# Where a small bonus row is loaded and spread in the first microseconds of an attention and FFN kernel

## The chip, the cores and the metric

The kernel runs on one core of a Trainium2 chip. The metric is device time in microseconds (us), as the median of several executions. A run's time is about 1.7 us longer than the profile's span of the same run. Times are compared with times and spans with spans.

Besides its time, each execution has on record the mean clock that the throttle granted TensorE.

## The reference

An RWKV-like attention with a decay w, a bonus u and a running state, for 4 batches, 8 heads, 768 steps and head width 48. An FFN follows, from width 384 to 2048 and back, over all 3072 tokens.

```python
for t in range(S):
    kt, vt, rt = k[:, :, t], v[:, :, t], r[:, :, t]
    cur = einsum('bhd,bhe->bhde', u[None] * kt, vt)          # the bonus: u counts for step t alone
    y[:, :, t] = einsum('bhd,bhde->bhe', rt, state + cur)
    state = w[None, :, :, None] * state + einsum('bhd,bhe->bhde', kt, vt)
x = y.transpose(0, 2, 1, 3).reshape(B * S, H * D)
h = x @ w_in
out = (h / (1 + exp(-h))) @ w_out
```

## The kernel before

The work is cut into 24 units (6 chunks of 128 steps, 4 batches each). The bonus of a unit is worked out in the natural layout: GpSimd multiplies k by u (`ku`), then r by that (`rku_f`), VectorE sums over the head's width, and the sums scale v. For this, u has to lie on all 128 partitions (`u_bc`). It is loaded as one small row, TensorE turns it to columns (`to_cols`), and four further transposes of the broadcast columns spread it (`to_rows`). The decay's powers, which `p1` multiplies into the transposed r and k, come from the row w, which goes the same way.

```python
    load_row(nc.sync, wrow, w)              # SP's queue
    load(0, (0,), nc.scalar)                # r of unit 0, ScalarE's queue
    load_row(nc.scalar, urow, u)            # u behind it
    load(0, (1,))                           # k of unit 0, SP's queue; all others follow there
    ...
    def spin(n, t=None):                    # dummy matmuls that keep TensorE's clock up
        ...
    spin(6)
    wT = to_cols(wrow, None)
    spin(3)
    ...
    def p1(i, spins=0, mid=()):
        ...
        for t, src in ((tr, rin), (tk, kin)):
            flat = src[n].rearrange("p h d -> p (h d)")
            for p in range(NP):
                nc.tensor.transpose(t[0:PR, p, :], flat[:, 128 * p:128 * p + PR], ident)
            if mid:
                mid.pop(0)()
        ...
    p1(0, mid=[cols_u, rows_u])             # u's columns between r and k, its spreading behind k
    p1(1)
    nat_ku(0)                               # GpSimd
    nat_rk(0)
    win_part(0, 512)                        # GpSimd issues a part of the weights
    nat_ku(1)
    nat_rk(1)
    ...
    p2(0, spins=2)
    bonus_sum(0)                            # VectorE reduces
    bonus_sum(1)
    ...
    p2(1)
    p3y(0)
    ...
    spin(4)
    p3y(1)
    p3e(1)
    spin(1)
    p4(0)
    p1(2)
    ...
```

## Time and profile before

| | before |
|---|---|
| median of 3 runs | 199.02 us (198.54 to 199.46) |
| span of the profile | 197.3 us |
| TensorE busy, idle | 189.2 us, 8.1 us |
| GpSimd's first bonus product starts | 8.19 us |
| its fourth (`rku_f` of unit 1) starts | 12.27 us |
| TensorE idle in 12 to 15 us | 1.81 us |

The change concerns the start, where everything stands behind GpSimd, whose four bonus products wait for `u_bc`. The lines are in the prediction below.

### The profile page before, as it was taken

What the parts mean: (1) busy time and instruction counts of PE and PEld (TensorE: products, weight loads), DVE (VectorE), ACT (ScalarE), POOL (GpSimd) and SP (SyncE); (2) the same over time, 40 slices, a digit from 0 to 9 for tenths busy, and PEclk for the clock granted to TensorE, in tenths of its full rate; (3) what the DMA queues carried; (4) which work ended last, traced back from release to release, by engine and by line L of the source; (5) the groups of instructions that cost most, each with busy time, mean ns of one, the idle gap of its engine ahead of it and who ended that gap; (6) DMA issues with size and microseconds to landing.
All of it is one profiled execution on the core that took longest, in us unless ns stands there. A gap on an engine that the chain in (4) does not pass through costs nothing.

```text
span 197.3 us, 4925 instructions
## 1 busy us (share of the span) xinstructions
PE 189.2 (96%) x1918; PEld 127.4 (65%) x1918; DVE 115.7 (59%) x233; ACT 91.0 (46%) x207; POOL 115.2 (58%) x145
## 2 busy tenths in 40 slices
PE   7969999899899999999999999999999999999993
PEld 2737878787666877675566766557666546644563
DVE  5867658885758764975675686476576344210121
ACT  3464587799311626215961216682016680069300
POOL 4389969989966859697669647735437710000000
PEclk9999999999999999999999999999999999999999
DMA  5999997999788754665567377526371011210022
GB/s 115 220 168 139 145 230 152 174 182 195 152 192 211 163 114 104 146 138 129 119 120 139 103 176 163 104 59 121 94 190 43 20 22 43 79 60 0 3 81 80
DMA packets 89696, 24.12 MB, mean 122 GB/s; under 512 B 82888, under 2 KB 89672, under 8 KB 89672
## 3 DMA queue, kind: packets, MB, share of 16 engines
q1 hardware_dynamic: 84940, 20.46, 48.1%
q0 software_dynamic: 3680, 3.15, 10.7%
q10 hardware_dynamic: 1052, 0.20, 0.5%
q8 instruction: 15, 0.25, 0.5%
q14 instruction: 9, 0.07, 0.1%
HBM read 20.45 MB, written 4.72 MB: 128 GB/s over the span
## 4 chain that ended last, share of the span: by engine, by line
PE 72%; POOL 11%; DMA 9%; issue 3%; SPq 1%; DVE 0%; POOLq 0%
PE ops L373 30%; PE hps L361 24%; DMA kin<-in_k_dram 9%; PE ae L270 8%; PE xs L245 4%; POOL ku L183 3%; POOL rku_f L189 3%; POOL kc L194 2%; PE y L296 2%; POOL win L416 2%; PE y L293 2%; POOL vu L206 1%; PE ops L387 1%; PE sps L312 1%; SPq L69 1%
## 5 line engine op out<-in xcount | busy, mean ns | idle before, releaser
L364 ACT ACTIVATE gT<-hps 128x256 f16<-128x256 f32 (+1 forms) x128 | 59.8, 494 | 50.5 <-PE hps L361 48.9
L361 PE MATMUL hps<-xT,win 128*128 128x256 f16 (+1 forms) x384 | 69.2, 326 | 0.2
L373 PE MATMUL ops<-wout,gT 128*128 128x384 f16 x368 | 63.8, 326 | 0.0
L361 PEld LDWEIGHTS <-win 128*128 128x128 f16 x384 | 35.4, 98 | 22.9 <-issue 0.7
L373 PEld LDWEIGHTS <-gT 128*128 128x128 f16 x368 | 34.7, 98 | 22.4
L279 DVE TENSOR_TENSOR am<-ae,maskM 128x512 f16<-128x512 f32 x24 | 16.6, 691 | 31.9 <-PE ao L272 31.8
L377 DVE COPY osb<-ops 128x384 f32<-128x384 f32 x23 | 12.7, 554 | 28.9 <-PE ops L373 28.7
L183 POOL TENSOR_TENSOR ku<-kin,u_bc 128x384 f32<-128x384 f32 x24 | 24.2, 1006 | 7.0 <-ACT u_bc L152 5.4
L270 PEld LDWEIGHTS ae<-rk 48*128 48x128 f32 x192 | 23.1, 187 | 7.3 <-issue 4.7
L206 POOL TENSOR_TENSOR vu<-vin,rku 128x384 f32<-128x384 f32 x23 | 19.1, 832 | 14.6 <-DVE rku L200 14.5
L272 PE MATMUL ao<-rk 48*128 48x128 f32 x192 | 27.5, 284 | 0.0
L270 PE MATMUL ae<-rk 48*128 48x128 f32 x192 | 27.5, 284 | 0.0
L256 DVE TENSOR_TENSOR rk<-xs,pif 112x512 f32<-112x512 f32 x40 | 25.6, 681 | 1.7 <-PE xs L245 1.7
L262 ACT CAST rT<-rk 112x512 f16<-112x512 f32 x20 | 12.3, 616 | 29.7 <-DVE rk L256 29.7
L189 POOL TENSOR_TENSOR rku_f<-rin,ku 128x384 f32<-128x384 f32 x24 | 24.1, 1004 | 1.9
L194 POOL TENSOR_TENSOR kc<-kin,lamC 128x384 f16<-128x384 f32 x24 | 24.0, 1004 | 0.0
L272 PEld LDWEIGHTS ao<-rk 48*128 48x128 f32 x192 | 23.1, 187 | 0.0
L303 DVE TENSOR_TENSOR y<-y,vu 128x384 f16<-128x384 f32 x24 | 13.4, 557 | 8.3 <-POOL kc L194 2.5
L326 POOL CAST stb<-st 112x384 f16<-112x384 f32 x12 | 6.1, 504 | 20.7 <-DVE st L321 20.7
L279 DVE TENSOR_TENSOR am<-ao,maskM 128x512 f16<-128x512 f32 x24 | 16.3, 680 | 0.0
L200 DVE TENSOR_REDUCE rku<-rku_f 128x8 f32<-128x384 f32 x24 | 13.2, 550 | 3.2 <-POOL rku_f L189 2.7
L296 PE MATMUL y<-v,am 128*128 128x48 f16 x192 | 12.2, 185 | 2.8 <-ACT st L452 1.5
(73 smaller groups left out, 170.5 us busy)
## 6 DMA issues: line engine op xcount, KB each, us to landing
kin<-in_k_dram SPq DMA_DIRECT2D x24, 192.0 KB, 3.4
vin<-in_v_dram SPq DMA_DIRECT2D x24, 192.0 KB, 3.7
rin<-in_r_dram SPq DMA_DIRECT2D x23, 192.0 KB, 3.4
out_dram<-osb SPq DMA_DIRECT2D x23, 192.0 KB, 1.9
win<-in_moe_w_in_dram POOLq DMA_DIRECT2D x4, 384.0 KB, 5.7
wout<-in_moe_w_out_dram POOLq DMA_DIRECT2D x2, 768.0 KB, 11.5
xT<-y SPq DMA_TRANSPOSE x18, 2.3
rin<-in_r_dram ACTq DMA_DIRECT2D x1, 192.0 KB, 2.7
```

The lines of the kernel that those rows point to most:

```text
L183: nc.gpsimd.tensor_tensor(out=L["ku"], in0=kin[i % NIN][:, :, 0:D], in1=u_bc, op=ALU.mult)
L189: nc.gpsimd.tensor_tensor(out=L["rku_f"], in0=rin[i % NIN][:, :, 0:D], in1=L["ku"], op=ALU.mult)
L194: nc.gpsimd.tensor_tensor(out=kc[i % NKC][:, :, 0:D], in0=kin[n][:, :, 0:D], in1=lamC, op=ALU.mult)
L206: nc.gpsimd.tensor_tensor(out=L["vu"], in0=vin[i % NIN], in1=L["rku"].unsqueeze(2).broadcast_to([128, H, D]), op=ALU.mult)
L256: nc.vector.tensor_tensor(out=rk[:, :, :, 64 * g:64 * g + 64], in0=xs[g][0:PR], in1=lam(g), op=ALU.mult)
L270: nc.tensor.matmul(ae[:, p, :], L["kT"][0:D, p, :], L["rT"][0:D, p, :], start=True, stop=True)
L272: nc.tensor.matmul(ao[:, p, :], L["kT"][64:PR, p, :], L["rT"][64:PR, p, :], start=True, stop=True)
L279: nc.vector.tensor_tensor(out=am, in0=a, in1=maskM.unsqueeze(1).broadcast_to([128, NP, C]), op=ALU.mult)
L296: nc.tensor.matmul(y[:, 2 * p + j, :], L["am"][j][:, p, :], v16[:, 2 * p + j, :], start=not sc, stop=(not sc or j == 1))
L361: nc.tensor.matmul(hps, win[:, q, ft * 128:(ft + 1) * 128], xts[sc][:, q, b0:b1, :].rearrange("p b t -> p (b t)"), start=(q == 0), stop=(q ...
L364: nc.scalar.activation(out=gts[sc][:, ft, b0 * C:b1 * C], in_=hps, func=AF.Silu)
L373: nc.tensor.matmul(ops, gts[sc][:, ft, b * C:(b + 1) * C], wout[:, ft, :], start=(ft == 0), stop=(ft == NFT - 1))
```

## The change

The intent is to have u spread before unit 0's own transposes, so that GpSimd starts earlier. u therefore goes first and alone on ScalarE's queue. r of unit 0, now needed later, goes behind w on SP's queue. The diff, cut to its core:

```diff
     load_row(nc.sync, wrow, w)
-    load(0, (0,), nc.scalar)
     load_row(nc.scalar, urow, u)
-    load(0, (1,))
+    load(0, (0, 1))
 ...
     spin(6)
     wT = to_cols(wrow, None)
-    spin(3)
+    spin(2)
+    ucol = to_cols(urow, nc.scalar.copy)
+    spin(2)
 ...
+    to_rows(u_bc, lambda p: ucol[:, p:p + 1].broadcast_to([PR, 128]))
 ...
-    p1(0, mid=[cols_u, rows_u])
+    p1(0)
```

More of the change, by code (lines that the diff above doesn't have):

```diff
@@ L62, in unit, with load @@
         return divmod(i, B)
-    def load(i, which=(0, 1, 2), queue=nc.sync):
+    def load(i, which=(0, 1, 2)):
         if i >= NU:
@@ L68, in load @@
         for t, src in [((rin, r), (kin, k), (vin, v))[x] for x in which]:
-            queue.dma_start(out=t[i % NIN][:, :, 0:D],
+            nc.sync.dma_start(out=t[i % NIN][:, :, 0:D],
                               in_=src[b, :, sc * C:sc * C + C, :]
@@ L215, in bonus_act, with p1 @@
                                  func=AF.Copy, scale=L["rku"][:, h:h + 1])
-    def p1(i, spins=0, mid=()):
+    def p1(i, spins=0):
         n = i % NIN
@@ L226, in p1 @@
                 nc.tensor.transpose(t[0:PR, p, :], flat[:, 128 * p:128 * p + PR], ident)
-            if mid:
-                mid.pop(0)()
         rk = wrk.tile([PR, 2, NP, C], FP, name="rk")
@@ L422, in wout_part @@
             in_=moe_w_out[1024 * g:1024 * g + 1024, :].rearrange("(f p) n -> p f n", p=128))
-    def cols_u():
-        live["u"] = to_cols(urow, nc.scalar.copy)
-    def rows_u():
-        to_rows(u_bc, lambda p: live["u"][:, p:p + 1].broadcast_to([PR, 128]))
-    p1(0, mid=[cols_u, rows_u])
+    p1(0)
     p1(1)
```

## The prediction

> **What bounds the kernel now.** I read the page's busy shares first, then the busy slices, then a table of all engines by stretch, the waits of TensorE and GpSimd, and the start in order of time. The first two say that TensorE is the bound nearly everywhere:
>
> ```profile
> PE 189.2 (96%) x1918; PEld 127.4 (65%) x1918; DVE 115.7 (59%) x233; ACT 91.0 (46%) x207; POOL 115.2 (58%) x145
> ...
> PE   7969999899899999999999999999999999999993
> ```
>
> TensorE is idle for only 197.3 - 189.2 = 8.1 us. The table by stretch (length, then busy time and count of each engine, last the clock, DMA share and GB/s) says where:
>
> ```profile
> 0.00:4.00 4.00, 2.74 (x7) 0.80 (x7) 2.03 (x15) 1.47 (x2) 1.99 (x14) 1.00 0.42 81
> ...
> 8.00:12.00 4.00, 3.65 (x52) 2.99 (x50) 3.26 (x6) 2.30 (x8) 3.71 (x4) 1.00 1.11 216
> 12.00:16.00 4.00, 2.08 (x21) 1.05 (x19) 2.65 (x5) 2.94 (x12) 3.23 (x6) 1.00 1.04 150
> ...
> 52.00:180.00 128.00, 128.00 (x1287) 82.61 (x1285) 76.18 (x143) 53.25 (x106) 73.14 (x85) 1.00 0.50 113
> ```
>
> From 52 to 180 us there is no gap at all, so the only thing a change of the start can do is bring that solid block forward or push it back. The largest gap is in the third row: 4.00 - 2.08 = 1.92 us, and a further 1.03 us of that row's busy time are four dummy matmuls that only keep the clock up. The front is therefore set by something else than TensorE. The start in order of time (start, duration, engine, line, what it writes and reads, and in brackets the idle time before it and its releaser) shows what:
>
> ```profile
> 1.28 1.22 ACTq L83 DMA_DIRECT2D urow<-in_u_dram  x1
> ...
> 3.93 0.25 PE L132 MATMUL cols<-ident,wrow 4*112 4x4 f32 x1
> ...
> 6.36 0.25 PE L132 MATMUL cols<-ident,urow 4*112 4x4 f32 x1
> ...
> 6.65 0.16 ACT L137 COPY cols_sb<-cols 112x4 f32<-112x4 f32 x1 [2.62 <-PE cols L132]
> ...
> 7.03 0.55 PE L150 MATMUL rows<-ident,cols_sb 112*128 112x112 f32 x4
> ...
> 7.62 0.49 ACT L152 COPY u_bc<-rows 128x384 f32<-128x384 f32 x1 [0.81 <-PE rows L150]
> ...
> 8.19 1.01 POOL L183 TENSOR_TENSOR ku<-kin,u_bc 128x384 f32<-128x384 f32 x1 [5.45 <-ACT u_bc L152]
> ...
> 12.27 1.00 POOL L189 TENSOR_TENSOR rku_f<-rin,ku 128x384 f32<-128x384 f32 x1
> ...
> 13.30 0.55 DVE L200 TENSOR_REDUCE rku<-rku_f 128x8 f32<-128x384 f32 x1 [1.54 <-POOL rku_f L189]
> ...
> 14.50 0.10 PEld L296 LDWEIGHTS <-am 128*128 128x128 f16 x1 [2.01 <-DVE am L279]
> ```
>
> The reader is to follow one chain: GpSimd stands still for 5.45 us until the bonus row u has been turned to columns, spread over the partitions and copied (u_bc). Its four products (ku, rku_f of units 0 and 1, with a weight transfer's issue between) then run without a gap from 8.19 to 13.27. VectorE waits 1.54 us for the last of them before its reduce, the masks of unit 1 stand behind that reduce in VectorE's order, and TensorE waits for the masks at 14.5. GpSimd goes on nearly without a gap to 34 us, issuing the weight parts and releasing the next loads at 20.2 us. So the bonus row's way to GpSimd is what sets the front.
>
> **What the Trainium skill says.** (1) "TensorE: Matmul & The Clock Gate", Part 1 (the HAM clock gate): the first some 3.4 us of activity run at half clock, a 512-column matmul every 426.7 ns, later every 215.7 ns. The trace agrees: the first dummies start at 1.26, 2.52, 3.37 and 4.94 us, steps of 0.42 each; unit 0's r transposes from 5.37 step by 0.21 us, those of its k from 6.54 by 0.11. So here the clock rises near 6.3 us, and the new order must be counted at half clock up to there. (2) "DMA: Bandwidth & Descriptors", Issuing engines are not separate DMA queues: transfers of all issuers run on the same 16 engines, so several issuers save only issue time. The trace fits: in 4 to 8 us, all but the first load on one queue, the engines are full (share 1.18, 229 GB/s). Moving r of unit 0 to the other queue costs its place in the order, not bandwidth. (3) "Perfetto Trace Analysis", DMA Instruction — HWDGE: the shown duration ends when the descriptors are made, not when data has landed. The trace agrees: the first r issues for 0.43 us and lands after 2.7.
>
> **The change part by part.**
>
> Loads. The u row's issue moves from 1.28 to 0.81 us, as w's is now. w is used at 3.93, right after the sixth dummy (3.37 + 0.43 = 3.80; the same 0.13 us of gap stands ahead of the u transposes at 6.36). An equal transfer issued with it has landed by about 4 us; it will be needed at 5.1, so no wait. r of unit 0 moves from 0.81 to 1.7 us, where k of unit 0 is now; k took 3.09 us to land (1.72 to 4.81), so r lands near 4.8, before its new use (below, 6.8). All other loads move back one place, 0.45 to 0.8 us (one load of 192 KB at about 250 GB/s is 0.8). k of unit 0 then lands near 5.5, its first use is after 7. The initial loads end near 13.3 instead of 12.5; nothing waits on them now and the slack (unit 2's r is first read at 14.7) is over 1 us.
>
> TensorE, from the w transpose at 3.93, which stays. Two dummies at 4.12 and 4.55, to 4.98; the u transpose at 5.11 (that 0.13 gap); two dummies at 5.30 and 5.72, to 6.15. ScalarE copies the columns 0.29 us after the transpose, at 5.40 to 5.56, under the dummies. The four spreading transposes begin at 6.15 instead of 7.03. Then r of unit 0: two spreading steps at 0.21 (half clock) and two at 0.11 make 6.79 instead of 5.37; its k at 7.23 (was 6.54), unit 1's r at 7.67 (was 7.42), k at 8.11 (was 7.86), the two dummies of the first products at 8.55 (was 8.29). One dummy more in all, 0.43 us at half clock, in time that was waiting anyway.
>
> GpSimd. Now it starts 8.19 - 7.03 = 1.16 us after the spreading starts. With about 0.15 for the half clock: 6.15 + 1.16 + 0.15 = 7.45. That is **0.74 us earlier**. Its four products and the issue take 13.27 - 8.19 = 5.08 us as before, so the last ends at 12.53.
>
> VectorE. The decay's powers end at 6.89 in either order, now followed at 7.03 by r's product. A tile's product follows its transposes' start by 16.39 - 15.75 = 0.64 us (unit 2), so r's comes at 6.79 + 0.64 = 7.43, **0.40 us later**. k's product at 8.04 ends at 8.72. The attention products need it and the dummies' end: 8.55 + (8.82 - 8.29) = 9.08 instead of 8.82, 0.26 later. The masks of unit 0 and its reduce follow 0.26 later, so VectorE is free at 11.75 + 0.26 = 12.0, still ahead of GpSimd's 12.53. The loss lies inside the 1.54 us of waiting and costs nothing; the reduce of unit 1 goes from 13.30 to 12.56. ScalarE's eight scalings end near 13.95, and y of unit 0 reads them at 14.2: no wait. The front so gains 0.74 us.
>
> Later. Weight part 1, loads 4 and 5 and the other weights are issued by GpSimd or after it, so they move forward with it. But the first weight part (issued 10.22, landed 6.8 us later, about 17.0) is used at once at 17.5, and the backlog of loads ends 0.8 later now. I take off 0.15 for that. Expected 0.74 - 0.15 = 0.6 us: 199.02 - 0.6 = **198.4 us**.
>
> **The rivals.**
>
> (a) The gain is swallowed by DMA. For: the chain that ended last contains a 15.24 us transfer of k:
>
> ```profile
> 36.02 15.24 DMA kin<-in_k_dram
> 51.30 0.43 PE xs L245 x8
> ```
>
> TensorE waited 0.55 us for it, in a stretch with DMA share 1.12. If that backlog doesn't move, all of the gain becomes a longer wait there. Against: in 19.5 to 20 us the DMA engines are idle (share 0.00), and all that makes the backlog is issued after, behind GpSimd. If it came so: 199.0.
>
> (b) The later r transposes govern. For: they move by 1.4 us, and attention by 0.26. Against: 1.54 us of waiting lie between. If GpSimd's gain failed as well (u landing late): 199.2 to 199.4.
>
> (c) More gain than counted: the clock rises earlier or dummies were a floor, so GpSimd starts 1.0 us sooner, and a shorter gap at 26 to 27 us (GpSimd waits 1.49 us there for unit 4's k) gives something too: 197.9. For: the k and weights compete less once they start earlier. Against: that wait is between two things that move together.
>
> **Range and chances.** The three runs of before spread over 0.92 us by themselves, more than the expected gain. The mechanism's outcomes reach from 197.9 to 199.4; weighting mine and (c) over (b), 8 in 10 lie in **197.7 to 199.2**. Two per cent is 4.0 us, half of all idle time of TensorE, and 1.92 of that is all the gap concerned: faster 0.01, within 2% 0.98, slower 0.01.
>
> **What would show each step.** The u transpose near 5.1 us and ku of unit 0 at 7.3 to 7.6 show the main step; a wait of TensorE at the u transpose shows a late row. r's product on VectorE at 7.4 shows the loss, the reduce of unit 1 at 12.5 that it is hidden. TensorE's gap in 12 to 16 us should shrink and the first y of unit 1 come at 13.8 instead of 14.5. If the later events (load of unit 4's r at 20.4, the k that landed at 51.3) come 0.6 earlier, the gain is carried to the end; if they stand where they were, (a) is right. A total above 199.3 or below 197.6 would prove me wrong, as would ku starting after 8 us.

## The result, and the profile after

| first comparison | before | after |
|---|---|---|
| median of 6 runs | 199.09 us | 197.70 us |
| range | 198.54 to 199.46 | 196.83 to 198.18 |
| ratio after / before | | 0.9926 [0.9902, 0.9951] |

A ratio is the mean time of one kernel's runs over that of the other's of the same rounds, so it is not quite the ratio of the medians. The bracket is its 95% interval.

The kernel is 0.7% faster, by 1.4 us instead of the 0.6 predicted. The median lies just on the lower end of the predicted range, and the gain is over twice the forecast.

In the page of the changed kernel, TensorE's busy time moved by 0.7 us (189.2 to 188.5), while the span is 2.2 us shorter:

```profile
span 195.1 us, 4926 instructions
...
PE 188.5 (97%) x1919; PEld 126.9 (65%) x1919; DVE 115.6 (59%) x233; ACT 91.1 (47%) x207; POOL 115.5 (59%) x145
...
PE   7979999899999999999999999999999999999993
```

The start in order of time (start, duration, engine, line, what it writes and reads, in brackets the idle time before it and its releaser):

```profile
4.65 0.21 PE L131 MATMUL cols<-ident,urow 4*112 4x4 f32 x1
...
5.24 0.55 PE L151 MATMUL rows<-ident,cols_sb 112*128 112x112 f32 x4
...
6.39 1.37 POOL L186 TENSOR_TENSOR ku<-kin,u_bc 128x384 f32<-128x384 f32 x1 [3.65 <-ACT u_bc L153]
...
7.03 0.69 DVE L232 TENSOR_TENSOR rk<-tr,pif 112x512 f32<-112x512 f32 x1
...
10.84 1.01 POOL L192 TENSOR_TENSOR rku_f<-rin,ku 128x384 f32<-128x384 f32 x1
...
11.88 0.55 DVE L203 TENSOR_REDUCE rku<-rku_f 128x8 f32<-128x384 f32 x1 [0.44 <-POOL rku_f L192]
```

GpSimd stands still for 3.65 instead of 5.45 us, and its fourth product starts at 10.84 instead of 12.27. VectorE waits 0.44 instead of 1.54 us for it. TensorE's gap in 12 to 16 us is smaller: 4.00 - 3.15 = 0.85 us of idle time, where it was 1.92. The block without a gap still has none from 60 to 180 us (length, busy time and count of each engine, clock, DMA share, GB/s):

```profile
12.00:16.00 4.00, 3.15 (x29) 1.86 (x27) 3.69 (x7) 3.44 (x13) 3.39 (x5) 1.00 1.12 198
...
60.00:180.00 120.00, 120.00 (x1187) 76.61 (x1186) 68.79 (x130) 52.78 (x105) 65.69 (x77) 1.00 0.45 104
```

So this pair of profiles shows the predicted mechanism at about twice the predicted size: 1.43 us at GpSimd's fourth product instead of 0.74. But it is a pair of single executions. The u transpose comes at 4.65 us here, and the two dummies ahead of it step by 0.21 us instead of the 0.42 that the prediction counted with. The clock rose sooner in this execution. Whether the change does that, or chance, one pair can't say.

### The profile page after: what moved, and what is told of

Same layout as the page of the kernel before. It is cut to its first block, busy times and chain, and to the rows that moved or that the text cites. A ratio compares the mean times of both kernels' runs of the same rounds, so it can differ in the third digit from the quotient of the medians.

```text
span 195.1 us, 4926 instructions
## 1 busy us (share of the span) xinstructions
PE 188.5 (97%) x1919; PEld 126.9 (65%) x1919; DVE 115.6 (59%) x233; ACT 91.1 (47%) x207; POOL 115.5 (59%) x145
## 3 DMA queue, kind: packets, MB, share of 16 engines
q0 software_dynamic: 3680, 3.15, 10.5%
## 4 chain that ended last, share of the span: by engine, by line
PE 79%; POOL 14%; issue 2%; DMA 2%; SPq 1%; DVE 1%; ACT 0%; POOLq 0%
PE ops L374 31%; PE hps L362 27%; PE ae L271 10%; PE xs L246 4%; POOL ku L186 3%; POOL rku_f L192 3%; POOL kc L197 3%; PE y L297 2%; POOL vu L209 2%; DMA kin<-in_k_dram 2%; PE y L294 2%; POOL win L417 2%; PE sps L313 1%; PE ops L388 1%; POOL sdec L329 1%
```

## The experiments

Theories put up against each other:

- **A, the start**: GpSimd's earlier start is carried one to one to the end, and all of the gain is this.
- **B, the queue**: the earlier u row, or the other order of the loads, gives part of it.
- **C, the clock**: TensorE's smaller gap spares drops of the clock that the kernel before suffers in some executions.
- **D, chance**: the clock's first rise falls at different times from run to run, and the first comparison caught a good draw.

Every kernel below was timed in six runs (the last in four), in rounds with the kernel before on the same chip; all gave the reference's result. There were four sets of rounds, on three chips, and the changed kernel was timed in the first (after_again) and the fourth (after_third) of them. The columns on the clock take from each run's record whether its mean clock was at 1.0 (0.998 to 1.000 is meant) or lower. The three kernels with an added tile are not in the table; their numbers stand in their sections.

| run | mean us | ratio to before [95%] | runs with clock 0.989 to 0.991 | mean of the runs at 1.0 | TensorE idle in 12 to 15 us of the profile |
|---|---|---|---|---|---|
| before, 44 runs beside the others, and before_again, before_third | 198.32 | | 15 of 56 | 198.00 (41 runs) | 1.81, 1.67, 1.50 |
| after (first comparison) | 197.60 | 0.9926 [0.9902, 0.9951] | 0 of 6 | 197.60 | 0.81 |
| after_again | 197.03 | 0.9937 [0.9901, 0.9973] | 0 of 6 | 197.03 | 0.73 |
| after_third | 197.19 | 0.9926 [0.9892, 0.9961] | 0 of 6 | 197.19 | 1.03 |
| only_order | 197.41 | 0.9951 [0.9916, 0.9986] | 0 of 6 | 197.41 | 0.91 |
| only_queue | 198.16 | 0.9988 [0.9948, 1.0028] | 1 of 6 | 197.96 | 1.89 |
| u_first | 197.18 | 0.9952 [0.9913, 0.9992] | 0 of 6 | 197.18 | 0.60 |
| before_gap_filled | 197.92 | 0.9981 [0.9936, 1.0027] | 0 of 6 | 197.92 | 0.24 |
| before_gap_filled_2 | 198.09 | 0.9994 [0.9956, 1.0031] | 0 of 6 | 198.09 | 0.52 |
| before_wide_gap | 199.82 | 1.0059 [1.0016, 1.0103] | 3 of 6, and 3 at 0.981 | none | 2.29 |
| after_wide_gap | 197.60 | 0.9947 [0.9914, 0.9981] | 1 of 6 | 197.48 | 1.46 |
| late_pool_same_tiles | 197.55 | 0.9962 [0.9929, 0.9994] | 0 of 6 | 197.55 | 1.59 |
| late_pool_same_tiles_filled | 197.72 | 0.9975 [0.9943, 1.0007] | 0 of 6 | 197.72 | 0.19 |

### The two kernels again

No edit. The first pair is measured once more, to see how much of the 1.4 us was the draw.

> The changed kernel once more, unedited, to get a second profile and more times. Clock theory: in the first profile of the changed kernel TensorE rose to full clock near 4.1 us, in that of before near 6.3, and nothing that was changed lies before 4.1 us, so this is chance; then ku of unit 0 starts anywhere from 6.4 (early clock) to 7.5 us (late clock), the time follows it, and the mean gain over before is 0.7 to 1.0 us (ratio 0.995 to 0.9965). Rival, the change itself brings the early clock: ku again at 6.4 us and the ratio again near 0.9926. Second rival, the gain beyond 0.74 us is a transfer wait that vanishes near 51 us: no wait of TensorE on k of unit 8 in this profile either, and the ratio near 0.9926 wherever ku starts.

> The kernel before, unedited, against itself: ratio 1.000 within 0.002 on every theory. Its profile is what counts. Clock theory: if the clock happens to rise early here, ku of unit 0 starts near 7.1 us instead of 8.19. Transfer theory: the wait of TensorE for k of unit 8 near 51 us, 0.5 us, shows again; if it is absent in this profile at the same time as an unchanged total, the wait is no part of the difference.

Measured: after_again 0.9937, with a median of 197.03 us. The kernel before, run as a candidate against itself, came to 0.9994 [0.9948, 1.004]. The gain is real and lies between 0.6 and 0.7% in both comparisons so far, and after_third, below, gives 0.9926 once more. In after_again the u transpose falls at 5.08 us, almost exactly where the prediction had it, and so do the first and the last product:

```profile
7.10 1.01 POOL L186 TENSOR_TENSOR ku<-kin,u_bc 128x384 f32<-128x384 f32 x1 [4.37 <-ACT u_bc L153]
...
11.18 1.00 POOL L192 TENSOR_TENSOR rku_f<-rin,ku 128x384 f32<-128x384 f32 x1
```

Before_again has its own surprise. GpSimd was 0.69 us earlier than in the first profile of the same kernel:

```profile
7.50 1.00 POOL L183 TENSOR_TENSOR ku<-kin,u_bc 128x384 f32<-128x384 f32 x1 [4.78 <-ACT u_bc L152]
...
11.58 1.00 POOL L189 TENSOR_TENSOR rku_f<-rin,ku 128x384 f32<-128x384 f32 x1
```

Nevertheless its span is the same to 0.1 us, 197.2 against 197.3. Something later took the lead away. In slices of 1 us (length, TensorE's busy time, clock, DMA share, GB/s):

```profile
12.00:13.00 1.00, 0.55 (x3) 1.00 1.08 165
13.00:14.00 1.00, 0.18 (x1) 1.00 1.06 169
14.00:15.00 1.00, 0.60 (x11) 1.00 1.22 218
15.00:16.00 1.00, 1.00 (x9) 0.62 1.14 209
16.00:17.00 1.00, 1.00 (x8) 0.50 0.98 148
17.00:18.00 1.00, 1.00 (x6) 0.50 1.22 203
18.00:19.00 1.00, 1.00 (x9) 0.68 0.42 74
```

After the gap the granted clock is at half for some 3.4 us, with TensorE fully busy. That takes 3.4 / 2 / 197.2 = 0.9% off the execution's mean clock, and that run's record says 0.991. So the mean clock on record, which all runs but those of before in the first comparison have, tells in which runs this happened. In the 56 runs of the kernel before that have such a record there are 15 with 0.989 to 0.991. Their mean is 199.19 us, against 198.00 for the 41 others. **A drop costs 1.2 us.** (The spans of the profiles, below, say the same.) The changed kernel has none in 18 runs, which at the same rate would come by chance in (41 / 56)^18 = 0.4% of cases.

### The two halves of the change

The order alone (the changed kernel with the old queues), and the queues alone (the kernel before with the new ones):

```diff
 # only_order, against the changed kernel
+    load(0, (0,), nc.scalar)
     load_row(nc.scalar, urow, u)
-    load(0, (0, 1))
+    load(0, (1,))
```

```diff
 # only_queue, against the kernel before
-    load(0, (0,), nc.scalar)
     load_row(nc.scalar, urow, u)
-    load(0, (1,))
+    load(0, (0, 1))
```

> Only the order on TensorE as in the changed kernel (bonus row turned and spread ahead of unit 0's r); the two issues on the ScalarE queue as before, r of unit 0 first, the bonus row second at 1.28 us. If the order makes the gain: within 0.3 us of the changed kernel, ratio near 0.993 to 0.995. If the row's place in the queue matters, TensorE waits for the row (landing near 4.3 to 4.9 us) and up to 0.4 us of the gain is lost.

> Only the queues as in the changed kernel; the order on TensorE as before. My account: ku of unit 0 still follows the old order (7.1 to 8.2 us by the clock), loads one place later, nothing gained: ratio 0.999 to 1.002. If the queues make the gain beyond 0.74 us (for instance by moving the later transfers), 0.995 to 0.997.

Measured: only_order 0.9951, only_queue 0.9988 with an interval around 1. The order in TensorE's program gains by itself, and the queues by themselves show no gain clear of noise. In only_order u is still behind r on ScalarE's queue, and yet TensorE takes it at 4.84 us with no wait in front, so the row had landed in any case:

```profile
4.84 0.21 PE L132 MATMUL cols<-ident,urow 4*112 4x4 f32 x1
```

Theory B is not needed. Whether the queues add a little on top of the order (197.41 against 197.14 of after_again in the same rounds, and against 197.31 in all 18 runs of the changed kernel) can't be told from the noise.

Only_queue also gives a comparison at nearly equal clock. Each trace keeps a record of the clock's changes. Counted from the first instruction, its first rise is at 5.61 us in the profile of only_queue and at 5.81 in that of after_again. The fourth product starts at 11.87 in the old order and at 11.18 in the new one:

```profile
11.87 1.00 POOL L188 TENSOR_TENSOR rku_f<-rin,ku 128x384 f32<-128x384 f32 x1
```

That is 0.69 us, close to the 0.74 worked out in the prediction.

### Putting the start back, without the order

GpSimd does an extra product of no use ahead of its four. Its start is late again, while TensorE's order stays the new one:

```diff
 # after_late_pool, against the changed kernel; after_late_pool_filled has spin(10) for spin(4) too
     p1(0)
     p1(1)
+    slow = cst.tile([128, 5, D], FP)
+    nc.gpsimd.tensor_tensor(out=slow, in0=u_bc[:, 0:5, :], in1=u_bc[:, 0:5, :], op=ALU.mult)
     nat_ku(0)
```

> The changed kernel with one extra product of 128 x 240 on GpSimd ahead of unit 0's ku, some 0.7 us: all of GpSimd's lead is given back, all else of the change stays. If GpSimd's start is what the change is worth, with the gap on TensorE and the clock drop that hang on it: the whole gain goes, ratio 0.998 to 1.001, and clock drops near 15 to 16 us come back in about half the executions. If the order on TensorE or the loads had a worth of their own: ratio near 0.995.

> The last kernel with the gap filled by ten dummies in place of four. Clock-drop theory: GpSimd is as late as before, but the clock does not drop: ratio 0.996 to 0.998, as the filled kernel before, and 0.4 to 0.8 us better than the last kernel. Rival: equal to the last kernel.

Measured: 1.0052 [1.0013, 1.0092] and 1.005 [1.0009, 1.0092], that is slower than the kernel before, although the fourth product starts at 11.45 and 11.36 us, as early as in the earliest profile of that kernel (11.40 in before_third). No run has a clock drop. This was a badly made experiment: the new tile also changed the place of other buffers. Pad_only, below, shows that such a tile alone costs more than what was to be measured. The pair was replaced by one that writes the product into a tile that is there anyway and is overwritten later:

```diff
 # late_pool_same_tiles, against the changed kernel; ..._filled has spin(10) for spin(4) too
     p1(1)
+    nc.gpsimd.tensor_tensor(out=lamC[:, 0:5, :], in0=u_bc[:, 0:5, :], in1=u_bc[:, 0:5, :],
+                            op=ALU.mult)
     nat_ku(0)
```

> The changed kernel with the extra 0.73 us product on GpSimd ahead of unit 0's ku, its result now put into a tile that is written again later, so that no tile moves (the first try with a new tile of 960 bytes per partition moved the load buffers, and its loads were slower from 4 us on, before the extra product ran: 189 GB/s at share 1.26 against 208 at 1.05). If GpSimd's start is the change's worth: the gain is given back, ratio 0.997 to 1.001, the reduce of unit 1 back at 12.5 to 13.3 us, and clock drops at 15 to 16 us in some executions. If the order on TensorE or the loads matter in themselves: near 0.994.

> The last kernel with ten dummies in place of four in TensorE's gap. If the clock drop is part of the cost: granted clock 1.00 throughout and 0.3 to 0.7 us faster than the last kernel. Rival: equal to it.

Measured: 0.9962 and 0.9975, with means of 197.55 and 197.72 us and no drop in either, so the second gained nothing over the first. In the two profiles the fourth product is back near its old place, at 12.03 and 12.26, and the spans, 196.3 and 196.5, answer to it:

```profile
7.40 0.59 POOL L428 TENSOR_TENSOR lamC<-u_bc 128x240 f32<-128x240 f32 x1 [4.67 <-ACT u_bc L153]
...
12.03 1.00 POOL L192 TENSOR_TENSOR rku_f<-rin,ku 128x384 f32<-128x384 f32 x1
```

But the two profiled executions are each the slowest of their six (198.04 and 198.23 us), and the clock rose late in them (6.41 and 7.26 us), which delays the product too. The extra product took 0.59 us instead of the 0.73 counted with. From GpSimd's first product to the fourth bonus product it is 12.03 - 7.40 = 4.63 us, against 11.18 - 7.10 = 4.08 in after_again, so the delay put in was 0.55 us and not the whole lead. The mean of the twelve runs, 197.63, lies 0.32 us above the 197.31 of the changed kernel, with a standard error of 0.13, and the changed kernel was not timed in these rounds. Theory A wanted 0.55. The direction is shown, the size is not.

### Filling and widening TensorE's gap

Six more dummies ahead of the y products of unit 1 fill the gap in the kernel before without touching the start. Three fewer widen it, in both kernels:

```diff
 # before_gap_filled and before_gap_filled_2, against the kernel before
-    spin(4)
+    spin(10)
     p3y(1)
 # before_wide_gap against the kernel before, after_wide_gap against the changed one
-    spin(4)
+    spin(1)
     p3y(1)
```

> The kernel before with ten dummy matmuls in place of four behind unit 0's y, so that TensorE's gap at 12.5 to 14.5 us holds 1.3 us more of dummy work; no order, no queue and no real work is changed. Clock-drop theory: in two of three profiles with the old order so far the granted clock fell to 0.50 for 3.4 us from 15.4 or 15.9 us on, after this gap, and in none of the three with the new order; the drop costs those runs up to 1.3 us. Then filling the gap prevents it: clock 1.00 throughout, no time above 199.0, mean gain 0.4 to 0.8 us, ratio 0.996 to 0.998, with GpSimd's start as before (7.1 to 8.2). Rival (only GpSimd's earlier start matters): ratio 1.000, or up to 0.2 us slower by the dummies that run over.

> The kernel before with the filled gap, a second time, because its first ratio (0.9981, 0.9936 to 1.0027) leaves 0 to 0.8 us open. Clock-drop theory: no drop in the profile, no time over 199.0, ratio 0.996 to 0.999. Rival: 1.000.

> The kernel before once more for a third profile. Ratio 1.000 within 0.003. Clock theory: where the first full-clock matmul comes near 5 to 5.9 us, the granted clock falls to 0.50 near 15.2 to 16.1 us (three windows of 3.41 us later); where it comes near 6.3 or near 4.2 to 4.6 it does not, and a profile of the last kind has a time near 197.3, as the fast executions of before have.

> The kernel before with one dummy in place of four behind unit 0's y: TensorE's gap there is 0.64 us wider, no real work moves. Clock-drop theory: more executions drop, most of them; a drop to 0.50 for 3.4 us near 15 to 17 us in the profile, span then the start of unit 1's rku_f plus 185.6; mean time 0.3 to 1.0 us over before, ratio 1.002 to 1.005. Rival, the gap's width doesn't matter: ratio 1.000.

> The changed kernel with one dummy in place of four, so that its gap is about as wide as that of the kernel before. Clock-drop theory: the drop now shows in the new order too, in about as many executions as in before (a third to a half): times up to 198.8, mean 0.4 to 0.7 us over the changed kernel, ratio to before 0.997 to 0.999. Rival: times as the changed kernel's, 196.8 to 198.2, ratio 0.994 to 0.996.

> The changed kernel once more. If the first 1.4 us was partly luck: ratio 0.9945 to 0.9965, times 196.8 to 198.2; span of the profile equal to the start of unit 1's rku_f plus 184.25 to 184.5, no drop. If 1.4 us is the true size: ratio 0.9926 again.

Measured, filled: 0.9981 and 0.9994, neither clear of 1 by the time alone. The record of the clock is clearer: no drop in 12 runs (at the rate of 15 in 56, twelve runs without one would come by chance in (41 / 56)^12 = 2% of cases), and a mean of 198.01 us over the twelve, where the 41 runs of the kernel before without a drop average 198.00. Filling the gap removes the drops, and the mean of the undisturbed runs stays where it was. Before_third, run beside the second of these, happened to have no drop in its six runs (0.9983 [0.9948, 1.0017]).

Measured, wide: the kernel before is slower, 1.0059 [1.0016, 1.0103]. All six runs have a low clock, three of them 0.981, which is twice the loss of one drop. Those three average 200.61 us, the three others 199.02. No profile fell on a double drop, so where the second one lies isn't known. The changed kernel with a wide gap has one drop in six runs, fewer than the third to a half expected, and at 0.9947 its ratio is in the range of the rival. The drop was in the profiled run, and it shows the same picture as before_again, about 1 us earlier:

```profile
12.00:13.00 1.00, 0.00 (x0) 1.00 1.20 191
13.00:14.00 1.00, 0.54 (x9) 1.00 1.21 220
14.00:15.00 1.00, 1.00 (x9) 0.69 1.20 221
15.00:16.00 1.00, 1.00 (x7) 0.50 0.77 112
```

For comparison, the stretch in the undisturbed after_again and in before_again, all engines:

```profile
16.00:20.00 4.00, 3.60 (x42) 2.69 (x41) 2.43 (x4) 2.62 (x7) 4.00 (x7) 1.00 1.02 152
```

```profile
16.00:20.00 4.00, 4.00 (x31) 2.75 (x30) 2.05 (x4) 1.67 (x4) 3.95 (x6) 0.67 0.78 113
```

In the same 4 us TensorE does 42 steps at clock 1.00 and 31 at clock 0.67, and looks busier in the second. A busy share of 100% is not a good sign by itself: read it with the clock beside it.

Over all kernels of the table, drops become more frequent with TensorE's idle time in 12 to 15 us. With 2.29 us of it all of 6 runs have one, with 1.46 to 1.89 in either order 17 of 74, and with 1.03 or less none of 48. (The idle time is that of the kernel's profiles. Counted are: in the middle class, the 56 runs of before, only_queue, after_wide_gap and late_pool_same_tiles; in the last one, the 18 of the changed kernel, only_order, u_first, and the 18 with a filled gap.) Theory C holds, and it is the width of the gap and not the order that does it. In 12 to 15 us no exact threshold can be given: before_third, with 1.50 us of idle time, kept its clock, and after_wide_gap, with 1.46, lost it.

The record of the clock in the traces sorts the profiles better. The first rise lies between 4.12 and 7.26 us. In all four profiles with a drop, the drop begins 10.24 us after that rise and lasts 3.41 us, a third of it. If each profile is cut into stretches of 3.41 us from its rise on (the first six were looked at), the stretch just before the drop holds 1.54, 1.67, 1.89 or 2.34 us of TensorE's idle time in these four. In the 13 others with such a record no stretch holds more than 1.50. In the first profile of before, an edge at 13.41 us split the gap. Before_third kept its clock (first line; 3.41 - 1.91 = 1.50) and after_wide_gap lost it at the end of the stretch (second line; 3.41 - 1.87 = 1.54):

```profile
11.49:14.90 3.41, 1.91 (x19) 0.88 (x18) 2.42 (x5) 2.96 (x11) 2.72 (x5) 1.00 1.17 201
```

```profile
10.96:14.37 3.41, 1.87 (x25) 1.20 (x26) 2.84 (x6) 3.00 (x11) 2.72 (x5) 1.00 1.15 189
```

So it matters how the gap falls into these stretches, and that follows the clock's first rise, as before_third's expectation had it (it rose at 4.66 us there, and the clock held). The sorting was found after the runs, from 17 profiles. No run was made to test it.

Where in the profile the clock is undisturbed, theory A can be read directly as the span less the start of the fourth product: 184.40 (before_third), 184.57 and 184.25 (gap filled), 184.26, 184.52 and 184.31 (the changed kernel, three times), 184.47 (u_first), 184.27 and 184.24 (late_pool_same_tiles and its filled form). The same remainder follows an early start and a late one, in both orders. With a drop it is 185.62 (before_again), 185.63 (only_queue), 185.55 and 185.68 (wide gaps). In the very first profile of before it was 185.03, without a drop: there TensorE waited for the k of unit 8, as the prediction had noticed. That wait is absent from before_third and from both profiles with the filled gap, so it does not belong to every execution, and neither does a 0.8 us wait for the second weight matrix in only_order (remainder 185.08).

### u before everything

One step further: the two dummies between w's and u's transposes are taken out.

```diff
 # u_first, against the changed kernel
     wT = to_cols(wrow, None)
-    spin(2)
     ucol = to_cols(urow, nc.scalar.copy)
     spin(2)
```

> The changed kernel without the two dummies between the w and the u transposes: u is turned at 4.15 us already if its row has landed. Then ku of unit 0 starts 0.4 (early clock) to 0.9 us (late clock) sooner, but VectorE's reduce of unit 1 can follow only to 11.8 us, where the masks of unit 0 end; gain over the changed kernel 0.2 to 0.4 us, ratio 0.990 to 0.992. If the row has not landed, TensorE waits for it and the ratio is that of the changed kernel, 0.993.

Measured: 0.9952 [0.9913, 0.9992], a mean of 197.18 us. It is as good as the changed kernel (197.31 in 18 runs) and no better. Its first product starts at 6.59 us but takes longer:

```profile
6.59 1.17 POOL L185 TENSOR_TENSOR ku<-kin,u_bc 128x384 f32<-128x384 f32 x1 [3.86 <-ACT u_bc L152]
```

It ends at 7.76. The same product in the first profile of the changed kernel started at 6.39 and took 1.37, so it too ended at 7.76, and in only_order 6.58 and 1.18 give 7.76 again. Where it started at 7.10 it took 1.01. So something holds it until 6.9 or so. In all of these VectorE works out the decay's powers just then, by products whose two inputs lie in SBUF:

```profile
4.51 2.38 DVE L162 TENSOR_TENSOR pif<-pif 112x8 f32<-112x8 f32 x7
```

They end at 4.51 + 2.38 = 6.89. The Trainium skill, "SBUF — State Buffer", section Who interferes with whom, says that a VectorE instruction with two SBUF inputs contends with a GpSimd instruction that reads SBUF. The three equal ends fit that, though no run here took the powers away to show it. If that reading is right, the powers are next in line, and spreading u still earlier is worth nothing while they stand where they are.

### A tile that nobody uses

```diff
 # pad_only, against the changed kernel
     p1(0)
     p1(1)
+    slow = cst.tile([128, 5, D], FP)
     nat_ku(0)
```

> The changed kernel with the unused tile of 960 bytes per partition and nothing else. If the place of the load buffers is what slowed the first late-GpSimd kernel: loads at some 190 GB/s and a DMA share of 1.2 to 1.45 in 4 to 8 us, TensorE waiting for unit 1's r and k, about 1.3 to 1.7 us slower than the changed kernel. If an unused tile is left out of the layout or its place is nothing: as the changed kernel.

Measured: in four runs beside before 1.0004 [0.9966, 1.0042]. The mean is 198.72 us, 1.5 us above after_third in the same rounds, with no clock drop. The tile is never written or read. It takes 960 bytes of each partition, and other buffers must then lie elsewhere (no trace shows which), and the first loads went slower. The line for 4 to 8 us of the changed kernel in its first profile, then of pad_only:

```profile
4.00:8.00 4.00, 3.76 (x27) 2.65 (x28) 3.40 (x11) 0.64 (x2) 1.54 (x2) 1.00 1.07 212
```

```profile
4.00:8.00 4.00, 4.00 (x23) 2.60 (x22) 3.01 (x10) 0.64 (x2) 0.52 (x1) 1.00 1.42 177
```

The DMA engines are busier (share 1.42 for 1.07) and move less (177 GB/s for 212). The three kernels with the tile all show it in this stretch (shares of 1.32 to 1.42, 176 and 177 GB/s), and none of the other 15 profiles does (1.02 to 1.18, 199 to 232 GB/s). This explains why after_late_pool lost more than its extra product is worth. Why the placement matters is not settled.

## Why the prediction was right or wrong

**The main step was right in mechanism, and in size as far as the profiles tell.** The u transpose was put near 5.1 us and `ku` at 7.45. In after_again and after_third they are at 5.08 and at 7.10 and 7.22; in the first profile, where the clock rose at 4.12 us, at 4.65 and 6.39. The gain of GpSimd was put at 0.74 us. At nearly equal clock it is 0.69 (only_queue against after_again). The times are less exact. In the two sets of rounds with the changed kernel, its 12 runs average 197.17 us and the 19 runs of before without a drop 198.16: 1.00 us, with a standard error of 0.16 from the spread of the runs. Over all runs it is 198.00 - 197.31 = 0.69 us (standard error 0.13), but that mean of before takes in two sets of rounds without the changed kernel.

**The step that failed is the sum under "Later".** It read "I take off 0.15" and "Expected 0.74 - 0.15 = 0.6 us", as if the rest of the kernel could only take away. Two terms of it were wrong:

- The 0.15 for the first weight part and the backlog of loads. The remainder after the fourth product is 184.26 to 184.52 us in the changed kernel and 184.25 to 184.57 in the old order, where undisturbed. Nothing is lost there.
- A term that was left out: the clock after TensorE's gap. The kernel before drops to half clock in 15 of 56 runs, at 199.19 - 198.00 = 1.18 us each (from the unrounded means). In the mean that is 15 / 56 x 1.18 = 0.32 us. The changed kernel drops in none of 18. With it the sum becomes 0.69 + 0.32 = 1.01 us instead of 0.6. (It equals the difference of the means of all these runs, 198.32 - 197.31, by arithmetic; that is no second proof.)

The prediction saw the gap of 1.92 us and said correctly that it would shrink, but read it as idle time only. The line for that stretch showed a clock of 1.00, and the one profile at hand happened to be of an execution without a drop. The spread of the three runs, 0.92 us, was taken for noise; in the later runs of before, part of the spread is this state.

**What the two terms leave open.** Against the kernel before in the same rounds, the changed kernel gained 1.47, 1.25 and 1.43 us (ratios 0.9926, 0.9937, 0.9926). Its repeats, at 197.03 and 197.15 us, lie below the 197.6 that the prediction had named as proof against it, and after_third's expectation had named 0.9926 as the sign that 1.4 us is the true size. So 0.2 to 0.5 us of these gains are in neither term. They may be noise, as the intervals reach 0.5 to 0.7 us to either side, or a third term; no run decides it.

**The clock's first rise was taken as fixed.** "So here the clock rises near 6.3 us" was about true of one execution (6.59 in its record, 5.3 us after the first dummy at 1.26, where the page's some 3.4 us was called in agreement). Over the profiles it lies anywhere from 4.12 to 7.26 us, and with it the fourth product of one and the same kernel moves by 0.45 us (10.84 to 11.29 in the changed kernel) or 0.87 (11.40 to 12.27 in the kernel before). The page cited in the prediction says in Part 1 that the window runs freely and that the count of slow matmuls varies from run to run, and the prediction did not draw on that. Theory D is true of the first pair of profiles, 4.12 against 6.59 us, whose products so lay 1.43 us apart. That the 1.4 us of the first comparison's times were a good draw is not shown: the two repeats gave nearly the same. Its six runs of before do average 199.07 us, where the rounds later gave 198.14 to 198.62, but the record holds no clocks for them, so how many were drops is not known.

**The rivals.** (a), a transfer that swallows the gain, was wrong: the k that landed at 51.30 is used at 49.17 with no wait. (b), the later transposes of r, was wrong: r's product is at 7.03 to 7.16, at most 0.13 us later than before. The predicted loss of 0.40 us did not come about in these executions, whose clock rose earlier than the 6.3 us that it was worked out with; in late_pool_same_tiles, with the same order and a rise at 6.41, the product is at 7.34. (c), more gain than counted, had the size nearly right but not the reasons: both kernels show early and late rises of the clock (4.12 to 6.05 us in the changed one, 4.66 to 6.59 before), dummies were not a floor, and the wait for unit 4's k stayed (1.49 before, 1.6 after).

**The signs named.** VectorE's reduce of unit 1 was put at 12.5 and is at 11.88 in the first profile, at 12.21 and 12.33 in the two others; `ku`, put at 7.3 to 7.6, starts before that in all three; the load of unit 4's r moved from 20.37 to 18.95, by the whole lead of the fourth product (1.42 of 1.43 us), and to 19.27 and 19.39 in the two others. The lead is carried on, as said.

**Still open**: the 0.2 to 0.5 us above, whether the line between 1.50 and 1.54 us of idle time in a stretch holds in other runs, where the second drop of before_wide_gap lies, and what the delayed products of late_pool_same_tiles cost.

## What to carry to other kernels

When a single small input gates an engine at the head of a long chain, look at the order in the producing engine's program before the queues: here the order alone gained and the queues alone showed no gain clear of noise. Treat an idle gap of TensorE as a risk to its clock as well as idle time, and read the granted clock of every run, since one profile can miss a state that a quarter of the runs are in. And when an experiment adds a buffer, run the buffer alone as a control: here an unused tile cost 1.5 us, as much as the whole change gained.

## What the Trainium skill lacked or had wrong

- "TensorE: Matmul & The Clock Gate", Why this matters for your kernels, advises against idle gaps over about 3 us between bursts, and Part 1 sets the fall to half clock after a whole idle window of about 3.4 us. Here the clock fell after much less: in before_again TensorE was idle for 1.67 us in 12 to 15 us, its longest wait there being 1.27 us, and the clock then was at 0.50 for some 3.4 us. In all, 17 of 74 runs dropped with 1.46 to 1.89 us of idle time in that stretch, none of 48 with 1.03 or less. How much idle time of a window is enough (here 1.54 us of 3.41, and not 1.50), and that a drop then comes in some runs only, is missing. Part 1 also puts the cost of the ramp at the start at under 1% of a typical span. A later drop costs about as little here (1.18 us of 198, 0.6%), but it is as large as what the whole change gains, and it can be avoided: six dummies more brought the drops from 15 of 56 runs to 0 of 12.
- No page that was read says that the place of a load's destination buffer in SBUF changes the speed of the transfer. Here an unused tile of 960 bytes per partition took the loads in 4 to 8 us from 212 GB/s at a DMA share of 1.07 to 177 GB/s at 1.42, and the kernel by 1.5 us.
